# A sequence mixer and a gated MLP on one core: sines from SiLU's table, a product written with channels innermost, and a new order

## The chip, the cores and the metric

The kernel runs on one core of one Trainium2 chip. A core has TensorE (PE, matmuls into PSUM), VectorE (DVE), ScalarE (ACT), GpSimd (POOL) and SyncE (SP, which here issues DMA transfers); each takes its own list of instructions in order, and semaphores hold an instruction until what it needs is done. The metric is the time of one execution in device microseconds.

## The reference

Two branches read the same input `x` of 2048 positions by 512 channels, and a sigmoid gate per position mixes them. Branch A is a long convolution: its kernel K is made from 128 complex modes a channel, as exp(l dt A) weighted by C and dt B, summed over the modes; the reference convolves by FFT. Branch B is a gated MLP with hidden width 1792. All of it is float32.

```python
P = jnp.exp(logdA[:, :, None] * l[None, None, :])       # l = 0..2047
K = jnp.einsum("dn,dnl,dn->dl", Cc, P, dB).real
Kf, Uf = rfft2(pad(K)), rfft2(pad(u))                    # zero-padded to 2 L
y = irfft2(Uf * Kf)[..., :L] + u * Dskip                 # branch A
h = _sigmoid(x @ w_gate) * (x @ w_up)
b = h @ w_down                                           # branch B
g = _sigmoid((x * gate_w).sum(-1, keepdims=True))
return g * y + (1 - g) * b
```

## The kernel before

**Branch B.** `load_x`, `load_gu` and `load_dn` bring inputs and weights from HBM into staging tiles (`st`, later also `parts`, which are pieces of tiles that branch A no longer needs). `split` halves each value into two fp32r numbers: ACT copies the rounded upper part (L1031), DVE subtracts it to get the rest (L1032). `hidden` multiplies in 12 matmuls a product (three pairings of halves, four chunks of channels, tile `gups`, 128x512, L1098). `post` takes the sigmoid of the gate as a tanh on ACT (`sg`, L1141), multiplies on DVE (L1143), and splits the result again into `h` (L1147, L1148). `down` multiplies `h` with `w_down` (`dps`, L1170), and `add` scales a result on ACT (`part`, L1189) and accumulates it in HBM, through SP for the first and POOL for later groups. `gates` makes the mixing gate with a tanh of four columns (L727).

**Branch A, K.** For 16 groups of 32 channels, `angles` and `magnitudes` build a table `B` of 64 powers of each mode, and for eight pairs of groups `powers` and `tables` build a table `T` by doubling: five times, the last e entries times one power give the next e (L575 to L577, e = 1, 2, 4, 8, 16). Angles go through `trig`: ACT makes the rounded turn (L474), DVE subtracts it, ACT takes an absolute value (L478) and two sines (L479 with a bias column `hpi` for the cosine, L481). Magnitudes are exponentials on ACT (L504, L547, L549). Sine and exponential lie in different activation tables, so ACT loads a table (ACT_TABLE_LOAD, 1283 ns) whenever the kind turns; in the version before, tanh is in the exponential's table and not in the sine's. `tables` multiplies `T` and `B` (tile `kps`, L619), `sort` evicts that to `kst` on ACT (L627), DVE adds `Dskip`, and `second` multiplies with a Fourier matrix (`wps`, L649): 64 matmul calls, which the compiler makes 128 instructions of 128 columns, on tiles of 32 rows by 64 columns of the array, eight of which run side by side. `wps` fills two pairs of PSUM banks, and two ACT evictions (L658) write it to `kev`, whose rows hold 16 channels a frequency; SP stores `kev` to `a_k` in HBM (L661). Four pairs make one half of K (`a_k_60`, then `a_k_61`).

**Branch A, the rest.** `rows` folds `x` and transforms it (`ups`, evicted to `evu`, stored to `a_u`). When a half of K is stored, `passes` loads `a_u` and `a_k` back, `ustep` (`s2u`), `kstep` (`s2k`), `inverse` (`ips`, evicted to `ev`, stored to `b_s`) and `finals`/`last` (`fps`) finish the convolution, and POOL or DVE adds it to the output. Copies marked `either` may stand on ACT or DVE.

**The order.** Every function above is a generator that yields steps; `Plan.run` reads a string, `ORDER`, letter by letter, and each letter picks the next step of one kind on one engine, for `either` the engine too. So the string sets the order of all engines' lists. `Plan.cost` holds the durations that give slots and due times; it issues nothing. The two evictions of `second`, as they stand before, are:

```python
dst = kev.rearrange("p k (i u s) -> p u s i k", i=2, u=2)[:, u]
te = yield "ACT", 1.8, lambda: A.activation(dst, ph[u].rearrange("p j s i k -> p (j s) i k"), AF.Copy), [t, kvs.t]
```

They read 128 frequencies in a row from PSUM and write each 16 floats (64 bytes) after the one before.

Of the kernel before, what the change touches and what calls it, by code (L numbers as in the profile page):

```python
# [32 lines left out]
P = 128  # L33
# [32 lines left out]
ORDER = (  # L66
    "ABDdeEfgZZEfGDdBgeZZEfgDdeZGVEfZBgDdeZWZWEfpgZZFDEudWfgZZhepvpAuvEWfEgZZDfCHugZZHpqXDIDJvIFdeZuKFdeiuhadeZKZLZMKvivahZMZ"
    "MNOMMGPXVEfKMuNPviuaSZwSZxPSSSvuSSZSPYVSvSSuQgRSSaaZZaEZfvwZgZauaSaSvRQrtxHuEZQZQvQwZtZaaSuuENOZPaZfvSNxSSTfrYVgEutPwKvE"
    "tWWUZZPvGHffPoaKLMQgZZZgZEKppuvuMRWWfpFuZvZaEfRpqMvMgZaZQQQuMurQTNOwUPZZKNMSutSvShoaaSaPSPSivSSuSZZPwaaaZZuSrgQRESjkwlvg"
    "StaaxaESxFRESxmfxQZwZfhaQQivvugQtmZZFhExgSNOSuPfZZavvuNnviZSgaZFEEhPituvaSSPZTwyUPuoZaaXQaIaRJXVIKHKwyZaRQLafMKaafZguwyv"  # L70
    "gUaaZaMQMYVQQNfZaOZTMuMKrvtvPNMwyuvSgSSKSKrZtEEYZtVtWWPWSSWuvPoaaaaZSjkPLSQSfrtMKtwyaupSpSZRSvMSfRQQQSSQSggNaaZurawtMZMy"
    "lmamtaZaOawyZZuESvvaZFPNpSphiSTavXFEaPuauZwyZPUPQXvZuvRZRQQQhQuFTZMKZoZhEENOVYZZVHrFtutrUvtMSPNSoZtfgfgSjSfZuvSZSiigaPkS"
    "hvPYVaZSuWZSPuvQSRRviSaaZSpSQwynZrWutWErtEttWQSfSZagZvQpuaaQSpNpSOawylaaaaZmuPNwPyZSPfaaXaSTawyPmZXVZUQogIvZuaaaJIKKaYst"
    "tZRwyaaaaLMKRQQQQrNTOVMfvnMtHZMwyMKgYPNUotauMSSKSSPSZPSZrPaDDSDjtSakrluZtZKvQSRRvSZZaSvZSQtZmmQdtQuvDuQNOnbbbbbb0veSuZwa"
    "ayavZZZPuNdePFuP1bb2ZSSvShvuaSiSdPFZSTZLM3ewUy45uKMFdhohvvubeZZaZZQRR6bub4MbZbH5iavZqDia6QZbQQQNOTuZMMPDdwyUZ6NKvPvMSSSS"
    "oaaSSubDdeajSZPSkuPdlZ6Swaa7eZuQSSmabbmb8DdnyRveSeZv!RSZZvE0!$wa$ZuuSQQQQSNOS!!$$ESyZaaw1baaaP2ZZuNPSSTwUbv345vZyPEbvZfg"
    "PQoaaaZZuvR6bRIbJ4u6bIKQbZbuQKLMywZaQaa5fgwQKMZaaT6MvaNObyM67wZU8fMKPoavqyNMaaSKZSSSjkPZSgwEaFaKxaEGfSub!vSuZ!$$SPSSgbyw"
    "aaPZSuQZSaS!b!x$vvSRlZRQQuvufQQSZwamLMKaaZmuNEMhOf0Sw1b$b3MSxZPNMgSvaZxaaZ24SgvZ56bbEPPTb4wbUZPZQuMuZZboababRRu5Z6ZaivEv"
    "KQbZQZbEbQQTv6xNOEwU67fgx8ZuMnPfNoaufaaZSSSSvgS!uZSP!$$vSvPwaaSaZSZESPSQgFuvhixSjSfFuvZSRZRgZQuvS!hQkQ!FhlZiQiZufgwaaamv"
    "NamnZSwaaaOPNP$aESuvP$SST0wP1bbZyZxUQuvoRRQQQQZaa2fgaZaZTuvZ34ZwUoj5bEb66akuvbb4auvaZawlmmnbbbbZZZuvbab56aZZyfEug6bvbbbZ"  # L80
    "7b8E#u!Eb#b$b$bav#Zfgbawuv013344$Zaaa56$56b66bZbb9buZE9bZy90bZafwbb71bb3g9Zu24bay8!b!Z$ZEfvf#4v#g%$05b66bEaZbZuE5bbg6vbb"
    "b&($bbZ)bb)f((**(6(**gZ0Za199f22a99Z$ZwauFaugv193399a7fvuEFaZu8!#4Z9hvg4Z$!%u$i%#5F&(6))((**fZZEbvu$f(h6g$999g(w&))b5v**"
    "ZiZuZb4Zav)((*9%*((hy**FcZha667iZbu&()i5)((**ca((**bcbZazZcaa6avaz8!!!6$aaaazZc#v4Z566$aubauauy7Zaz8a!ya$v#u$c!av!aZzaav"
    "$$Zavu$azZu$999aaa9%ZZc&()aycZaZua9aFaF)v(v(**F999%&9h99u(9%&ia(*zvvu(h*vhiazia99aaaa()aaza)(a(az)z*99))c)%&a)c)cz(ca)a)"
    "z)c)*aaaa(a(a*z))acaazczc*")

# [90 lines left out]
class Plan:  # L177


    def __init__(self):  # L180
# [134 lines left out]
def body(ctx, tc, xp, xt, prm, ldt, dsk, gw, wgu, wdn, c_wu, c_wf, c_wk, c_wwk, c_wwu, c_wwv, c_pw, out):  # L315
# [115 lines left out]
    def preludes():  # L431

        yield E["dt"]
        for k in range(NG // NQ):
# [31 lines left out]
            quads[k][0].set(t)  # L466

    def trig(shape, f, cs, t):

# [8 lines left out]
        t = yield "ACT", act(n), lambda: A.activation(af, f, AF.Abs), [t]  # L478
        t = yield "ACT", ("sin", act(n) + 0.1), lambda: A.activation(cs, af, AF.Sin, scale=-2 * math.pi, bias=hpi), [t]  # L479
# [151 lines left out]
    def second(q, kss, kst, kready):  # L631
# [7 lines left out]
        banks = yield XB, 2  # L639
        ph = [b.tile("wps", [P, 2, 2, 2, P]) for b in banks]  # L640

        def mms():
            for i in range(2):
                for s in range(2):
                    for h in range(2):
                        for x in range(0, 4, 2):
                            for jj in range(4):
                                r = slice(32 * jj, 32 * jj + 32)
                                mm(ph[jj // 2][32 * x:32 * x + 64, jj % 2, s, i], kst[r, i, h, 4 * s + x:4 * s + x + 2], wk[r, h],  # L649
                                   start=(h == 0), stop=(h == 1), tile_position=(32 * jj, 32 * x), skip_group_check=True)  # L650
# [5 lines left out]
        for u in range(2):  # L656
            dst = kev.rearrange("p k (i u s) -> p u s i k", i=2, u=2)[:, u]
            te = yield "ACT", 1.8, lambda: A.activation(dst, ph[u].rearrange("p j s i k -> p (j s) i k"), AF.Copy), [t, kvs.t]  # L658
            banks[u].free(te)
# [59 lines left out]
    def gates(t4):  # L719
# [6 lines left out]
        def work():  # L726
            A.activation(g[:, c], gl[:, c], AF.Tanh, scale=0.5)  # L727
# [409 lines left out]
    def post(half, sb, f, pp):  # L1137
        (pg_, bg, tg), (pu, bu, tu) = pp
        ss, = yield SG, 1
        sg = ss.tile("sg")  # L1140
        t = yield "ACT", ("exp", actp(512)), lambda: A.activation(sg, pg_, AF.Tanh, scale=0.5), [tg, ss.t]  # L1141
        bg.free(t)
# [125 lines left out]
```

## Time and profile before

| | us |
|---|---|
| median of three runs | 648.88 |
| lowest and highest run | 645.97, 654.21 |
| profiled execution, its own time | 644.45 |
| span of that execution, first to last instruction | 642.7 |
| transfers of that execution | 105.50 MB, mean 164 GB/s |

In the profile an engine's busy time is the union of its instructions. Rows of waits say who waited for whom: engine, tile and line, the releaser, total, number and longest in microseconds. Rows of groups give the line, the operation, `out<-in` with shapes, the count, busy microseconds, the mean of one in ns, and idle time ahead. "PEld" are weight loads, which run beside matmuls. The chain of waits is the chain of work that ended last.

### The profile page before, as it was taken

To read this page: it belongs to the slowest core of one execution; us is meant where nothing else is said; L and a number is where in the kernel's file an instruction comes from. 1 tells how busy PE (TensorE), PEld (TensorE's weight loads), DVE (VectorE), ACT (ScalarE), POOL (GpSimd) and SP (SyncE) were. 2 spreads that over 40 slices of the span, in tenths; PEclk is the share of its full clock that TensorE was granted. 3 is DMA by queue.
4 is the path that set the end of the run, shared out by engine and by line. 5 is a ranking of instruction groups with operands and counts; after the bars stand their busy time and mean duration, and the time that the engine had idled before them with its cause. 6 is when DMAs were issued, how large, how long until landed. Compare 5 with 4: busy or idle time off the path is not lost.

```text
span 642.7 us, 16774 instructions
## 1 busy us (share of the span) xinstructions
PE 603.5 (94%) x7145; PEld 451.9 (70%) x7145; DVE 548.5 (85%) x784; ACT 431.3 (67%) x650; POOL 49.9 (8%) x61
## 2 busy tenths in 40 slices
PE   7999989899998997998999999989999987998987
PEld 3667778677876875866776777767776664676755
DVE  5999889999999999999999899998657652985367
ACT  4595998789898599789966899587642332442130
POOL 0000000011100110000010100000100010242021
PEclk9999999999999899899999999999999987999989
DMA  7504624439634628589488346735489999998986
GB/s 246 174 33 115 197 68 160 143 48 229 149 100 157 164 35 234 161 179 210 96 165 173 69 124 157 217 105 156 72 193 253 233 240 276 256 208 187 239 177 164
DMA packets 94650, 105.50 MB, mean 164 GB/s; under 512 B 39664, under 2 KB 65136, under 8 KB 93552
## 3 DMA queue, kind: packets, MB, share of 16 engines
q1 hardware_dynamic: 86512, 92.89, 53.1%
q0 software_dynamic: 8064, 11.54, 13.0%
q8 instruction: 56, 0.92, 0.6%
q14 instruction: 18, 0.15, 0.1%
HBM read 61.41 MB, written 42.99 MB: 162 GB/s over the span
## 4 chain that ended last, share of the span: by engine, by line
DVE 37%; PE 24%; ACT 14%; DMA 13%; issue 7%; SPq 4%; POOL 1%; DVEq 0%; POOLq 0%; ACTq 0%
PE gups L1098 10%; PE dps L1170 9%; DVE t L575 3%; DVE T L576 3%; DMA parts<-b_s 3%; DVE T L577 3%; DVE h L1148 2%; DVE sg L1143 2%; DVE gu L1032 2%; ACT B L547 2%; DMA parts<-a_u 2%; DVE B L556 2%; DMA st<-wgu 2%; DVE dnw L1032 2%; DVE ex L475 2%
## 5 line engine op out<-in xcount | busy, mean ns | idle before, releaser
L1098 PE MATMUL gups<-x,gu 128*128 128x512 f32 x1344 | 338.2, 399 | 5.7 <-ACT sg L1141 1.5
L1098 PEld LDWEIGHTS gups<-x,gu 128*128 128x128 f32 x1344 | 251.4, 190 | 77.3 <-issue 8.5
L1170 PE MATMUL dps<-dnw,h 128*128 128x512 f32 x672 | 176.8, 400 | 6.0 <-DVE h L1148 2.8
L1170 PEld LDWEIGHTS dps<-dnw,h 128*128 128x128 f32 x672 | 125.6, 190 | 45.2 <-issue 7.5
L1194 POOL DMA_DIRECT2D out<-part x31 | 27.8, 896 | 452.1 <-ACT part L1189 437.9
L1147 ACT ACTIVATE h<-sg 128x512 fp32r<-128x512 f32 x56 | 34.7, 627 | 32.7 <-DVE sg L1143 18.6
L547 ACT ACTIVATE B<-B 128x32 f32<-128x32 f32 (+2 forms) x96 | 53.5, 672 | 0.3
L1189 ACT ACTIVATE part<-dps,omg 128x512 f32<-128x512 f32 x47 | 32.0, 682 | 22.6 <-PE dps L1170 22.4
L1148 DVE TENSOR_TENSOR h<-sg,h 128x512 fp32r<-128x512 f32 x56 | 38.2, 684 | 7.6 <-ACT h L1147 7.5
L575 DVE TENSOR_TENSOR t<-T,bz 128x1024 f32<-128x1024 f32 (+3 forms) x48 | 41.2, 859 | 1.9 <-ACT ez L479 0.7
L577 DVE TENSOR_TENSOR T<-T,t 128x1024 f32<-128x1024 f32 (+3 forms) x48 | 41.5, 864 | 0.7
L1143 DVE SCALAR_TENSOR_TENSOR sg<-sg,gups 128x512 f32<-128x512 f32 x56 | 37.5, 679 | 5.3 <-ACT sg L1141 5.3
L576 DVE TENSOR_TENSOR T<-T,bz 128x1024 f32<-128x1024 f32 (+3 forms) x48 | 41.3, 860 | 0.0
L619 PEld LDWEIGHTS kps<-B,T 128*32 128x32 f32 x2048 | 29.4, 110 | 12.2 <-ACT part L1189 9.7
L1031 ACT ACTIVATE gu<-st 128x512 fp32r<-128x512 f32 (+1 forms) x49 | 29.1, 606 | 12.2 <-DMA st<-wgu 12.0
L619 PE MATMUL kps<-B,T 128*32 128x64 f32 x2048 | 31.9, 220 | 5.3 <-ACT part L1189 4.9
L1032 DVE TENSOR_TENSOR gu<-st,gu 128x512 fp32r<-128x512 f32 (+1 forms) x49 | 32.0, 661 | 3.0 <-ACT gu L1031 3.0
L1141 ACT ACTIVATE sg<-gups 128x512 f32<-128x512 f32 x56 | 33.1, 591 | 0.8 <-PE gups L1098 0.6
L658 ACT ACTIVATE kev<-wps 128x1024 f32<-128x1024 f32 x16 | 30.9, 2003 | 3.1 <-PE wps L649 3.1
L340 ACT ACTIVATE ev<-ips 128x512 f32<-128x512 f32 x23 | 13.2, 597 | 27.9 <-PE ips L879 19.9
L479 ACT ACT_TABLE_LOAD x23 | 29.5, 1283 | 0.4
L340 ACT ACTIVATE yt<-fps 128x512 f32<-128x512 f32 x7 | 4.2, 597 | 32.2 <-PE fps L954 32.2
(129 smaller groups left out, 728.7 us busy)
## 6 DMA issues: line engine op xcount, KB each, us to landing
st<-wgu SPq DMA_DIRECT2D x45, 256.0 KB, 4.8
a_u<-evu SPq DMA_DIRECT2D x32, 256.0 KB, 4.3
a_k<-kev SPq DMA_DIRECT2D x8, 1024.0 KB, 4.9
b_s<-ev SPq DMA_DIRECT2D x32, 256.0 KB, 4.4
out<-part POOLq DMA_DIRECT2D x31, 256.0 KB, 4.4
ak<-a_k SPq DMA_DIRECT2D x28, 256.0 KB, 6.1
parts<-b_s SPq DMA_DIRECT2D x24, 256.0 KB, 8.0
st<-wdn SPq DMA_DIRECT2D x23, 256.0 KB, 4.7
```

The costliest lines, as they stand in the source:

```text
L547: A.activation(B[:, :, 0, 1 << k::2 << k], B[:, :, 0, 1:64 >> k:2], AF.Exp, scale=float(1 << k))
L575: yield "DVE", c, lambda: V.tensor_tensor(t2, src, sb, op=OP.mult), [t, slot.t]
L576: te = yield "DVE", c, lambda: V.tensor_tensor(dst, src, br, op=OP.mult), [t]
L577: te = yield "DVE", c, lambda: V.tensor_tensor(dst, dst, t2[:, :, ::-1], op=OP.add), [te]
L619: mm(p[32 * jj:32 * jj + 32, s], T[:, 32 * i + ch, c], B[:, ch, c], start=(c == 0), stop=(c == 1), tile_position=(0, 32 * jj), skip_group_ ...
L1032: te = yield "DVE", dve(n), lambda: V.tensor_tensor(lo, st, hi.bitcast(F32), op=OP.subtract), [te]
L1098: mm(p, gu[:, a, k, dc], x[:, b, dc], start=(dc + n == 0), stop=(dc == NC - 1 and n == 2))
L1141: t = yield "ACT", ("exp", actp(512)), lambda: A.activation(sg, pg_, AF.Tanh, scale=0.5), [tg, ss.t]
L1143: t = yield "DVE", dve(512), lambda: V.scalar_tensor_tensor(sg, sg, 1.0, pu, op0=OP.add, op1=OP.mult), [t, tu]
L1147: t = yield "ACT", act(512), lambda: A.activation(h[:, 0], sg, AF.Copy), [t, hs.t]
L1148: t = yield "DVE", dve(512), lambda: V.tensor_tensor(h[:, 1], sg, h[:, 0].bitcast(F32), op=OP.subtract), [t]
L1170: mm(p, h[:, a, 128 * s:128 * s + 128], dn[:, b], start=(f == fs[0] and n == 0), stop=(f == fs[-1] and n == 2))
```

## The change

1. The sines: `sine` issues, when the plan has just turned to the sine's kind, a SiLU of one column into a new tile `lead`, so that the table loaded is SiLU's, and then the sine without a load of its own. Tanh lies in that table too, so `post` and `gates` no longer declare a kind, and a tanh follows either table.
2. `second` writes its product with the four values of a frequency (i, s) innermost: each matmul's 128 columns lie 4 floats apart in PSUM. The evictions read two neighbours (s) from one bank, two from the other (j), and write those four next to each other in `kev`.
3. `split` takes its size as an argument (512, or 256 for the first weights); the planner's durations for a table turn (1.48 with the SiLU), the evictions (1.0) and the tanh change.
4. `ORDER` is another string throughout.

```diff
-    "ABDdeEfgZZEfGDdBgeZZEfgDdeZGVEfZBgDdeZWZWEfpgZZFDEudWfgZZhepvpAuvEWfEgZZDfCHugZZHpqXDIDJvIFdeZuKFdeiuhadeZKZLZMKvivahZMZ"
+    "BAEfgBDdeZZEEfDdegZZBGDdeGVWfpgZZWEpfWgDdpeZZWApEXfgZZDdeDEfguvZuHdHIJvCIKEfgZKLEfZgZuZDdFhMKiaMMMZevuFXhVFeZMYVNOKvDdeZ"
...
+    lead = cst.tile([P, 1], F32, name="lead")
...
-            return n[1] + (1.28 if n[0] != self.kind else 0.0)
+            return n[1] + ((1.48 if n[0] == "sin" else 1.28) if n[0] != self.kind else 0.0)
...
-                        self.kind = m[0]
+                        self.turned, self.kind = m[0] != self.kind, m[0]
...
+    def sine(dst, src, **bias):
+        if plan.turned:
+            A.activation(lead, hpi, AF.Silu)
+        A.activation(dst, src, AF.Sin, scale=-2 * math.pi, **bias)
...
-        t = yield "ACT", ("sin", act(n) + 0.1), lambda: A.activation(cs, af, AF.Sin, scale=-2 * math.pi, bias=hpi), [t]
+        t = yield "ACT", ("sin", act(n) + 0.1), lambda: sine(cs, af, bias=hpi), [t]
...
-        t = yield "ACT", ("sin", act(n)), lambda: A.activation(f, f, AF.Sin, scale=-2 * math.pi), [t]
+        t = yield "ACT", ("sin", act(n)), lambda: sine(f, f), [t]
...
-        ph = [b.tile("wps", [P, 2, 2, 2, P]) for b in banks]
+        ph = [b.tile("wps", [P, 2, P, 2, 2]) for b in banks]
...
-                                mm(ph[jj // 2][32 * x:32 * x + 64, jj % 2, s, i], kst[r, i, h, 4 * s + x:4 * s + x + 2], wk[r, h],
+                                mm(ph[jj // 2][32 * x:32 * x + 64, jj % 2, :, i, s], kst[r, i, h, 4 * s + x:4 * s + x + 2], wk[r, h],
...
-            dst = kev.rearrange("p k (i u s) -> p u s i k", i=2, u=2)[:, u]
-            te = yield "ACT", 1.8, lambda: A.activation(dst, ph[u].rearrange("p j s i k -> p (j s) i k"), AF.Copy), [t, kvs.t]
+            dst = kev.rearrange("p k (i u j s) -> p u k i j s", i=2, u=2, j=2)[:, u]
+            te = yield "ACT", 1.0, lambda: A.activation(dst, ph[u].rearrange("p j k i s -> p k i j s"), AF.Copy), [t, kvs.t]
...
-        t1 = yield "ACT", ("exp", 0.6), work, te
+        t1 = yield "ACT", 0.6, work, te
...
-        t = yield "ACT", ("exp", actp(512)), lambda: A.activation(sg, pg_, AF.Tanh, scale=0.5), [tg, ss.t]
+        t = yield "ACT", actp(512), lambda: A.activation(sg, pg_, AF.Tanh, scale=0.5), [tg, ss.t]
```

Two places of the engines' lists show what the new string and the tables do. Line numbers of the changed kernel are six or seven higher below `sine`. The first is ACT, about the third of the four `gates`. Before:

```order
L1141 ACTIVATE sg<-gups 128x512
L479 ACT_TABLE_LOAD
L479 ACTIVATE ez<-af,hpi 128x384
L727 ACT_TABLE_LOAD
L727 ACTIVATE g<-gl 128x4
L728 ACTIVATE omg<-g 128x4
L729 ACTIVATE g<-g 128x4
L1141 ACTIVATE sg<-gups 128x512
L481 ACT_TABLE_LOAD
L481 ACTIVATE ez<-ez 128x384
L504 ACT_TABLE_LOAD
L504 ACTIVATE ey<-ey 128x320
```

The same stretch of work in the changed kernel (`ez` and its exponential `ey`, L511):

```order
L1147 ACTIVATE sg<-gups 128x512
L472 ACT_TABLE_LOAD
L472 ACTIVATE lead<-hpi 128x1
L473 ACTIVATE ex<-af,hpi 128x32x32
L481 ACTIVATE af<-ez 128x384
L473 ACTIVATE ex<-ex 128x32x32
L1195 ACTIVATE part<-dps,omg 128x512
L485 ACTIVATE af<-ez 128x384
L473 ACTIVATE ez<-af,hpi 128x384
L1037 ACTIVATE x<-st 128x512
L473 ACTIVATE ez<-ez 128x384
L511 ACT_TABLE_LOAD
```

Four loads stood among the sines of one `ez` and its exponential; now two stand there, and the sines of an `ex` and an `ez` share the first. Over the whole list it is 49 loads before and 43 now.

The second place is SP, from the last store of `kev` on, where the second half's loads begin. Before:

```order
L661 DMA a_k_61<-kev 128x2048
L775 DMA wwu<-c_wwu 128x256
L784 DMA parts<-a_u 64x4x256 x4
L791 DMA wwk<-c_wwk 128x256
L1028 DMA st<-wgu 128x512
L796 DMA ak<-a_k_61 64x16x64 x2
L791 DMA wwk<-c_wwk 128x256
L796 DMA ak<-a_k_61 64x16x64 x2
L1028 DMA st<-wgu 128x512
L1028 DMA parts<-wgu 128x512
```

In the changed kernel, from two weight loads ahead of that store:

```order
L1034 DMA st<-wgu 128x512 x2
L668 DMA a_k_61<-kev 128x2048
L782 DMA wwu<-c_wwu 128x256
L791 DMA au<-a_u 64x4x256 x2
L791 DMA parts<-a_u 64x4x256 x2
L798 DMA wwk<-c_wwk 128x256
L803 DMA parts<-a_k_61 64x16x64 x2
L798 DMA wwk<-c_wwk 128x256
L803 DMA ak<-a_k_61 64x16x64 x2
L906 DMA b_s_62<-ev 64x1024
```

Weight loads (`wgu`, 256 KB each) have moved from behind that store to ahead of it: to the end of the list nine follow it before, and four now.

More of the change, by code (lines that the diff above doesn't have):

```diff
@@ L71 @@
[L71 to L82, printed above, removed]
@@ new lines @@
+    "ZNSEvpSTfMpfuwUxgvfZpPHPrttuPQgvgZiuZZvZRRuEfpoaaqauZQQQgQTvNMvKZOwxfUrPNMSSuZoSvZSEPSjukavPSSSaZuvSPtaQZSgZuvlwxRZSaZaR"
+    "SZZmaQQuvSQQSZfwaaFaFtSEtuvZNhOimFSZPZNuvZguvhiSXSfPwZaPhiuavZEfaZZPSauTZwEfXVgUEQoYVIaayaaZZfuZErtntvJRIKgKLHRQMKtQQgQN"
+    "vgwaaaaMMOyZMwyaaaaTZMKfgPNuvwUruvxytMSSSSZYVZoEajatkSPZSWuvSaPKSSrtWKLWatEWPZZZruMSlQRSpRSwapSvKaQQQyQaaumfgNvSSpOMZwaZ"
+    "aaMaZmPwSNauvZEZaaayyFSExuZvZftShiPPSTFuvpwyXZFPMuhiUQMhivZoRRZZnEFXZVgQZfEfuvYVuZZvZaQuvhiQaurvQattuvTNgOafwytUgKPNMSSS"
@@ L87 @@
+    "a*)a)aaza)ac))z)czc((**azc")
 XLATE = 0
@@ L1057, in load_gu @@
                         src = wgu[f].rearrange("p (k c m) -> p k c m", k=2, c=NC)[:, :, k]
-                        yield from split("splitw", src, gu[:, 0, :, k], gu[:, 1, :, k], gs, ready)
+                        yield from split("splitw", src, gu[:, 0, :, k], gu[:, 1, :, k], gs, ready, 256)
                         if k == 0:
```

24 lines of the change are left out of this document (15 added, 9 removed).

## The prediction

> **What bounds the kernel now.** I read the head of the profile first, then the busy time of each engine in three stretches, and then what TensorE (PE) waited for in each of them, because PE is the engine with the largest share.
>
> ```profile
> span 642.7 us, 16774 instructions
> ...
> PE 603.5 (94%) x7145; PEld 451.9 (70%) x7145; DVE 548.5 (85%) x784; ACT 431.3 (67%) x650; POOL 49.9 (8%) x61
> ```
>
> The columns of the next rows are stretch, length, and the busy microseconds of PE, PE's weight loads, DVE, ACT and POOL, then granted clock, DMA share and GB/s.
>
> ```profile
> 0.00:60.00 60.00, 53.17 (x234) 36.66 (x235) 51.51 (x105) 37.27 (x62) 0.73 (x5) 1.00 0.42 132
> 60.00:500.00 440.00, 422.55 (x5626) 325.77 (x5625) 408.95 (x554) 350.77 (x508) 24.51 (x28) 0.99 0.60 151
> 500.00:642.70 142.70, 127.83 (x1289) 89.50 (x1287) 87.99 (x126) 43.22 (x80) 24.69 (x28) 0.95 0.98 218
> ```
>
> PE is idle for 642.7 - 603.5 = 39.2 us: 6.8 at the start, 17.5 in the long middle stage, 14.9 in the last stage. The middle stage is tight on two engines at once: PE has 17.5 us free of 440 and DVE 31. ACT has 89 us free there, so on average it bounds nothing. But a share is an average, and the waits say where it matters. In the middle stage (columns: total, times, longest):
>
> ```profile
> PE kps L619 <- ACT part L1189: 4.9, 4, 1.9
> PE dps L1170 <- DVE h L1148: 2.5, 2, 1.7
> PE wps L649 <- ACT evu L340: 2.0, 2, 1.4
> PE wps L649 <- ACT ev L340: 2.0, 2, 1.4
> PE gups L1098 <- ACT sg L1141: 1.3, 2, 0.9
> PE dps L1170 <- ACT kst L627: 1.2, 1, 1.2
> ```
>
> The four ACT rows that free a bank (part, evu, ev, kst) and the sigmoid row sum to 4.9 + 2.0 + 2.0 + 1.3 + 1.2 = 11.4 us. So 11.4 of PE's 17.5 idle microseconds in the middle stage end with an ACT instruction. They fall in places where ACT is full, such as 230 to 260 us, with ACT busy for 29.54 of 30:
>
> ```profile
> 230.00:260.00 30.00, 26.64 (x520) 20.08 (x519) 29.24 (x50) 29.54 (x45) 2.62 (x3) 0.95 0.60 158
> ```
>
> In the last stage PE waits for DMA instead:
>
> ```profile
> PE fps L954 <- DMA parts<-b_s: 5.2, 6, 2.6
> PE s2u L817 <- DMA parts<-a_u: 3.8, 5, 2.0
> PE s2k L844 <- ACT ev L340: 1.7, 1, 1.7
> ```
>
> So ACT time is worth something only where it stands ahead of PE, and no rearrangement can win more than PE's idle time.
>
> **Terms of the change on ACT.** The groups of ACT instructions, shapes apart (busy, mean ns):
>
> ```profile
> L658 ACT ACTIVATE kev<-wps 128x1024 f32<-128x1024 f32 x16 | 30.9, 2003 | 3.1 <-PE wps L649 3.1
> L479 ACT ACT_TABLE_LOAD x23 | 29.5, 1283 | 0.4
> L547 ACT ACTIVATE B<-B 128x512 f32<-128x512 f32 x16 | 19.1, 1192 | 0.0
> L340 ACT ACTIVATE evu<-ups 128x1024 f32<-128x1024 f32 x15 | 15.3, 1018 | 0.0
> L1031 ACT ACTIVATE x<-st 128x512 fp32r<-128x512 f32 x16 | 10.1, 630 | 5.1 <-DMA st<-xt 5.0
> L727 ACT ACTIVATE g<-gl 128x4 f32<-128x4 f32 x4 | 0.8, 200 | 1.1 <-DVE ju L714 1.0
> ```
>
> The eviction kev moves 1024 values from PSUM in 2003 ns, where evu moves as many in 1018. It writes single values 64 bytes apart. The L547 row with 512 values, written 16 bytes apart, shows the same price: 1192 ns against 630 for 512 contiguous values. The new form writes four neighbours (16 bytes) at a time. Its reads change too: two neighbours in one PSUM bank, then two in the other. For runs of two the nearest rows are the doubling steps on DVE:
>
> ```profile
> L340 DVE COPY ev<-ips 128x512 f32<-128x512 f32 x9 | 6.1, 688 | 9.8 <-PE ips L879 4.9 <-DMA out<-mn 3.0 <-ACT ev L340 1.8
> L340 DVE COPY uf<-s2u 128x1024 f32<-128x1024 f32 x4 | 4.9, 1217 | 0.0
> L576 DVE TENSOR_TENSOR T<-T,bz 128x256 f32<-128x256 f32 x8 | 3.4, 420 | 0.0
> L576 DVE TENSOR_TENSOR T<-T,bz 128x128 f32<-128x128 f32 x8 | 3.3, 407 | 0.0
> L459 DVE TENSOR_TENSOR pg<-pg 128x128 f32<-128x128 f32 x8 | 1.9, 283 | 0.0
> ```
>
> The first step has single values 128 bytes apart and costs 407 ns for 128 values, against 283 contiguous; the second has runs of two and costs 420 for twice as many. Runs of two carry no penalty there, in SBUF. I take kev at 1018 ns, and keep 2003 (reads from alternating banks as slow as the old writes) as the other end; better than 1018 is excluded, since 1018 is the contiguous copy. Term: 16 x (2003 - 1018) = 15.8 us less on ACT, or 0.
>
> Table loads: ACT's instruction list has 49 before and 43 after, because sigmoids and the gates no longer turn the table away from the sines. That is 6 x 1.283 = 7.7 us less. What one switch costs in all is seen where four loads follow one another:
>
> ```profile
> 292.71 0.57 ACT L1141 ACTIVATE sg<-gups 128x512 f32<-128x512 f32 x1
> 293.30 1.28 ACT L479 ACT_TABLE_LOAD   x1
> 294.59 0.62 ACT L479 ACTIVATE ez<-af,hpi 128x384 f32<-128x384 f32 x1
> 295.22 1.28 ACT L727 ACT_TABLE_LOAD   x1
> 296.51 0.20 ACT L727 ACTIVATE g<-gl 128x4 f32<-128x4 f32 x1
> ```
>
> From the end of the sigmoid (293.28) to the start of the sine (294.59) pass 1.31 us, of which the load is 1.28: nothing else is paid. The Trainium skill ("ScalarE: Activation LUTs", What ACT_TABLE_LOAD costs) adds a drain of about 1380 ns to each load, 2.66 us a switch; by it six fewer would give 16 us, an estimate, but this trace does not show the drain, so the sum stays with 1.28.
>
> Added: 21 one-column SiLUs (lead), each right behind a load. The nearest row is L727 with four columns, 200 ns: 21 x 0.20 = 4.2 us more, queued ahead of the sine and whatever ACT holds behind it. Copies that either engine may do have also moved: counted in the two lists, DVE gives up one evu, three s2u evictions and one ev, and takes two yt. That is 4 x 1.22 + 0.69 - 2 x 0.69 = 4.2 us off DVE, and about 4 x 1.02 - 0.6 = 3.5 us on ACT. The sines and the splits keep their work; the planner's numbers for them issue nothing.
>
> ACT in sum: -15.8 - 7.7 + 4.2 + 3.5 = -15.8 us. ACT is not the bound, so this is worth only what PE stops waiting. Between 0 (other instructions in front of the same evictions take over) and 11.4 I take 7: the ends of those waits lie in full stretches, where a load or a kev stands in front, but DVE is as full there (29.24 of 30 above) and is late next. The 4.2 us off DVE are counted in this 7, against the 2.5 us that PE waits for DVE's h.
>
> **PE.** The product wps now writes its 128 columns 16 bytes apart. No row of this trace has a matmul with a strided output. The chain of waits shows it gapless, and shows a mode change:
>
> ```profile
> 469.30 2.03 PE wps L649 x125
> ...
> 484.68 1.37 PE gups L1098 x6
> ...
> 486.73 1.42 PE s2u L817 x61
> 488.16 1.59 PE gups L1098 x6
> ```
>
> wps sends 128 instructions of 128 columns through eight tiles at once: 2048 columns in 2.03 us, 0.99 ns each. gups streams 6 x 512 columns in 1.37 us, 0.45 ns each. So in wps each column already has twice the time for its write. That is why I take 0; fewer than 0 is excluded, since the same columns still pass. The other end is ACT's doubling for 16-byte steps (1192 against 630, x 1.9): 2.03 x 0.9 = 1.8 us a product, 8 x 1.8 = 14.6 us. The cover is that slack per column; without it PE, the fullest engine, pays in full. The Trainium skill ("Advanced Engine Details and Errata", PSUM Cachelines) says that any non-contiguous PSUM pattern slows matmuls significantly and wants every two consecutive elements adjacent. By that rule the outer end would hold; no run here shows it yet.
>
> The new order goes 63 times from the large products to small ones, before 58. The first gups behind a small product takes 1.59 instead of 1.37, so five more returns cost 5 x 0.22 = 1.1 us.
>
> **The last stage.** The last a_k store leaves behind two kev evictions, so K's second half can start about 2 us earlier. And the queue SP has moved: after the last a_k store there were nine weight loads (wgu) still to issue, now four. They compete there with what PE waits for:
>
> ```profile
> 475.05 0.33 SPq L661 DMA_DIRECT2D a_k<-kev  x1
> 476.12 3.31 SPq L784 DMA_DIRECT2D parts<-a_u  x4
> 480.18 0.38 SPq L1028 DMA_DIRECT2D st<-wgu  x1
> ```
>
> ```profile
> 500.00:550.00 50.00, 43.62 (x571) 28.55 (x569) 25.39 (x34) 16.00 (x27) 3.54 (x4) 0.90 1.15 247
> ```
>
> Five loads of 256 KB are 1.3 MB, 5.3 us of transfer at 247 GB/s. PE's waits for transfers in the last stage are 5.2 + 3.8 = 9.0 us. The loads moved ahead run beside a middle stage at 0.60 DMA share, so they are hidden there; without that cover the 5.3 us come back. Between 0 and 5.3 I take 2, since the three PE waits for b_s and a_u have queues of their own in front. The number of POOL's accumulating stores is unchanged.
>
> **Sum.** -7 + 0 + 1.1 - 2 = -8 us, against the profiled execution's own 644.45 us (span 642.7 and 1.75 around it): 636.5. That execution lies 4.4 below the median of 648.88 (645.97 to 654.21). The change alone puts the median at 641. I take the middle, 639.
>
> **Rivals.**
> *The strided product is slow.* Place: the eight wps. Price 8 x 1.8 = 14.6 us, so 644.5 - 8 + 14.6 = 651, from the median 655.5. It turns the change slower than before from 1.0 us a product on, and slower by 2% (13 us) from (13 + 8) / 8 = 2.6 us on. For it: no row of a strided output; against it: 0.99 ns a column. Chance 0.15. The rule of the Trainium skill quoted above would give this case.
> *ACT's relief is hidden.* kev stays at 2003 because its reads now alternate banks, or DVE, full in the same stretches, takes over every wait. Then ACT gains nothing that PE sees: -2 + 1.1 = -1, 644 to 648. For it: ACT's 89 free us; against it: the 11.4 us of waits. Chance 0.17.
> *More than forecast.* The order closes all of PE's ACT waits and its DMA waits of the last stage: -11.4 - 9.0 - 1.7 + 1.1 = -21 us, 623.5 to 628, about 626; halfway to it, 632. Against it: the granted clock of 0.90 and the DMA share of 1.15 in 500 to 550 stay. Chance 0.17.
> The forecast, 633 to 646, has 0.51.
>
> **How the numbers follow.** The range, 629 to 655, leaves out the better half of the last rival and the worse half of the first. Faster by over 2% (below 636; about what a measurement of this kernel can tell from no change): 0.17 and a fifth of the forecast's 0.51, 0.27. Slower by over 2% (above 662): a third of the strided case and a little of the hidden one, where an order laid out for a short kev meets a long one, 0.09. Within: 0.64.
>
> **What would show it.** kev near 1.0 us and 43 loads of 1.28; a lead near 0.2; wps near 2.0 in the chain (3.8 for the first rival); PE's waits for part, evu, ev and kst below 5 us in the middle stage; fewer PE waits for b_s and a_u. I am wrong if wps is longer, if kev stays at 2, or if PE's idle time is still 39 us with the waits under new names.

## The result, and the profile after

| | before | changed |
|---|---|---|
| median, us (runs) | 648.93 (4) | 630.68 (4) |
| lowest to highest | 645.97 to 654.21 | 627.29 to 633.48 |
| profiled execution, us | 644.45 | 627.29 |
| PE idle in the span, us | 39.2 | 29.3 |

The ratio of the times is 0.971 (95% interval 0.962 to 0.979): the change makes the kernel about 3% faster. Of the kernels below, only the one with SiLU's table and the loads moved back had executions in a slower state, two of six (630.12 and 630.96 us): its median counts them, its ratio doesn't. The page of the changed kernel, its head:

```profile
span 625.5 us, 16787 instructions
...
PE 596.2 (95%) x7145; PEld 447.3 (72%) x7145; DVE 542.6 (87%) x781; ACT 414.4 (66%) x668; POOL 49.9 (8%) x61
```

To see where the time went, I cut both executions at the same event, the last store of `kev`, which stands at 475.05 us before and at 459.59 after. The first 60 us are the start, from there to the store is the middle stage, the rest is the last stage. Columns as in the prediction: stretch, length, busy PE, weight loads, DVE, ACT, POOL, then clock, DMA share, GB/s. Before:

```profile
60.00:475.05 415.05, 397.60 (x5323) 308.00 (x5322) 390.31 (x532) 345.18 (x499) 24.51 (x28) 0.99 0.57 144
475.05:642.70 167.65, 152.78 (x1591) 107.27 (x1589) 106.63 (x148) 48.81 (x90) 24.69 (x28) 0.96 0.99 225
```

And the changed kernel:

```profile
60.00:459.59 399.59, 391.69 (x5287) 304.83 (x5286) 383.68 (x527) 328.20 (x514) 24.51 (x28) 1.00 0.59 147
459.59:625.50 165.91, 151.26 (x1605) 105.25 (x1603) 106.49 (x147) 45.98 (x87) 24.66 (x28) 1.00 1.04 224
```

The middle stage is 415.05 - 399.59 = 15.5 us shorter, the last stage 1.7 us. In the middle stage DVE's busy time falls by 6.6 us and its idle time, length less busy, from 24.7 to 15.9. PE's idle time there falls from 17.5 to 7.9.

The groups of ACT's instructions of the changed kernel (busy, mean ns, idle ahead):

```profile
L665 ACT ACTIVATE kev<-wps 128x1024 f32<-128x1024 f32 x16 | 15.9, 1021 | 2.0 <-PE wps L656 2.0
L472 ACT ACT_TABLE_LOAD x21 | 26.9, 1283 | 0.4
L556 ACT ACT_TABLE_LOAD x14 | 18.0, 1283 | 0.3
L511 ACT ACT_TABLE_LOAD x7 | 9.0, 1283 | 0.1
L1037 ACT ACT_TABLE_LOAD x1 | 1.3, 1283 | 0.7 <-PEq L1261 0.7
L472 ACT ACTIVATE lead<-hpi 128x1 f32<-128x1 f32 x21 | 4.3, 203 | 0.2
```

`kev` has lost half its time, and the 43 loads are there. Note where they stand: 14 at L556, the first exponential that makes `B`; before, that line (L549 there) had four, and twelve stood at the sigmoids. PE's waits of the middle stage that end with ACT:

```profile
PE kps L626 <- ACT part L1195: 1.9, 3, 0.8
PE gups L1104 <- ACT sg L1147: 1.7, 1, 1.7
PE wps L656 <- ACT evu L340: 1.2, 1, 1.2
...
PE dps L1176 <- ACT part L1195: 0.7, 2, 0.5
```

They sum to 5.5 us. Before, all rows of this kind sum to 12.0 (the prediction's 11.4 leaves out two small ones). Everything that the prediction asked to see of ACT is here. That reading is consistent, and the experiments show that it is wrong.

### The profile page after: what moved, and what is told of

Same layout as the page of the kernel before. It is cut to its first block, busy times and chain, and to the rows that moved or that the text cites. A ratio compares the mean times of both kernels' runs of the same rounds, so it can differ in the third digit from the quotient of the medians.

```text
span 625.5 us, 16787 instructions
## 1 busy us (share of the span) xinstructions
PE 596.2 (95%) x7145; PEld 447.3 (72%) x7145; DVE 542.6 (87%) x781; ACT 414.4 (66%) x668; POOL 49.9 (8%) x61
## 4 chain that ended last, share of the span: by engine, by line
PE 36%; issue 23%; DVE 14%; DMA 14%; ACT 7%; SPq 3%; POOL 2%; POOLq 0%; DVEq 0%; ACTq 0%
PE gups L1104 18%; PE dps L1176 11%; DMA b_s<-ev 3%; PE kps L626 2%; POOL out L995 2%; DMA ak<-a_k 2%; ACT B L554 2%; DMA st<-wdn 2%; DMA st<-xt 2%; PE wps L656 1%; DMA parts<-b_s 1%; DVE T L583 1%; PE s2k L851 1%; DVE T L584 1%; DMA au<-a_u 1%
## 5 line engine op out<-in xcount | busy, mean ns | idle before, releaser
L1104 PEld LDWEIGHTS gups<-x,gu 128*128 128x128 f32 x1344 | 250.1, 189 | 77.9 <-issue 10.5
L1176 PEld LDWEIGHTS dps<-dnw,h 128*128 128x128 f32 x672 | 123.4, 188 | 43.3 <-issue 6.9
L1037 ACT ACTIVATE gu<-st 128x512 fp32r<-128x512 f32 (+1 forms) x49 | 29.3, 605 | 10.8 <-DMA st<-wgu 10.0
L626 PEld LDWEIGHTS kps<-B,T 128*32 128x32 f32 x2048 | 29.3, 110 | 8.6 <-ACT part L1195 4.2
L481 ACT ACTIVATE af<-ex 128x1024 int32<-128x1024 f32 x16 | 16.9, 1055 | 16.8 <-DVE ex L532 16.8
L559 DVE TENSOR_TENSOR B<-B,ex 128x1024 f32<-128x1024 f32 x16 | 19.6, 1224 | 9.1 <-ACT B L554 8.9
L472 ACT ACT_TABLE_LOAD x21 | 26.9, 1283 | 0.4
```

The source lines that it names most:

```text
L626: mm(p[32 * jj:32 * jj + 32, s], T[:, 32 * i + ch, c], B[:, ch, c], start=(c == 0), stop=(c == 1), tile_position=(0, 32 * jj), skip_group_ ...
L1104: mm(p, gu[:, a, k, dc], x[:, b, dc], start=(dc + n == 0), stop=(dc == NC - 1 and n == 2))
L1176: mm(p, h[:, a, 128 * s:128 * s + 128], dn[:, b], start=(f == fs[0] and n == 0), stop=(f == fs[-1] and n == 2))
```

## The experiments

**Which edit did it.** The change has three edits that can be made apart: the new `ORDER`, the product and eviction of `kev`, and the sines. (The planner's new numbers go with the edits they describe, and `split`'s size with the string; they issue nothing, but the planner's durations choose which staging tile a load takes.) Six kernels fill in the combinations between the kernel before and the changed one. One theory says that ACT's shorter work is what PE got; its rival says that the order did it.

*The new order alone*: the new string, with `wps`, `kev` and the sines as they were.

```diff
-    "ABDdeEfgZZEfGDdBgeZZEfgDdeZGVEfZBgDdeZWZWEfpgZZFDEudWfgZZhepvpAuvEWfEgZZDfCHugZZHpqXDIDJvIFdeZuKFdeiuhadeZKZLZMKvivahZMZ"
+    "BAEfgBDdeZZEEfDdegZZBGDdeGVWfpgZZWEpfWgDdpeZZWApEXfgZZDdeDEfguvZuHdHIJvCIKEfgZKLEfZgZuZDdFhMKiaMMMZevuFXhVFeZMYVNOKvDdeZ"
...
```

> The new order with the old sines (their own table, 45 loads) and the old wps and kev (2.0 us an eviction). Theory A (the two edits free ACT ahead of PE, in whichever order): the order alone keeps less than a third of the gain of 18 us, 640 to 648 us, since it was laid out for evictions of 1.0 us and PE waits for ACT again by 10 us or more in the middle stage. Theory B (the order does it, ACT's relief is hidden): 630 to 636 us, with PE's waits for ACT in the middle stage at 4 to 6 us as in the changed kernel.

*`kev` alone*, on the kernel before:

```diff
-        ph = [b.tile("wps", [P, 2, 2, 2, P]) for b in banks]
+        ph = [b.tile("wps", [P, 2, P, 2, 2]) for b in banks]
...
-            dst = kev.rearrange("p k (i u s) -> p u s i k", i=2, u=2)[:, u]
+            dst = kev.rearrange("p k (i u j s) -> p u k i j s", i=2, u=2, j=2)[:, u]
```

> The old order and sines, with only wps and kev in the new layout. All theories: kev near 1.02 us, wps about 2.05 us in the chain. Theory A: 16 us less on ACT take a good part of PE's waits for ACT away, 638 to 644 us. Theory B: 646 to 650 us, no change.

*The sines alone*, on the kernel before:

```diff
+        if plan.turned:
+            A.activation(lead, hpi, AF.Silu)
+        A.activation(dst, src, AF.Sin, scale=-2 * math.pi, **bias)
...
-        t = yield "ACT", ("exp", actp(512)), lambda: A.activation(sg, pg_, AF.Tanh, scale=0.5), [tg, ss.t]
+        t = yield "ACT", actp(512), lambda: A.activation(sg, pg_, AF.Tanh, scale=0.5), [tg, ss.t]
```

> The old order and kev, with only the sines on SiLU's table (45 loads before the order changes them, and as many leads as turns). ACT has 4 x 1.28 = 5.1 us less of loads and about 20 x 0.2 = 4 us more of leads. Theory A: 646 to 649 us, about nothing. Theory B: 646 to 650 us. A clear gain here would show that the place of a load matters (ahead of a sigmoid), not the sum.

*Both edits in the old order*: the two diffs above together.

> The old order with both edits. Theory A: most of the gain, 634 to 640 us. Theory B: 645 to 650 us. Theory C (a gap of PE costs more than its length, because the granted clock falls behind it): whatever gaps of 1.4 us or more go, the mean clock rises with them, and the time falls by about twice the idle time that goes.

*The changed kernel without the `kev` edit*:

```diff
-        ph = [b.tile("wps", [P, 2, P, 2, 2]) for b in banks]
+        ph = [b.tile("wps", [P, 2, 2, 2, P]) for b in banks]
...
-            dst = kev.rearrange("p k (i u j s) -> p u k i j s", i=2, u=2, j=2)[:, u]
+            dst = kev.rearrange("p k (i u s) -> p u s i k", i=2, u=2)[:, u]
```

> The changed kernel with the old wps and kev layout (2.0 us an eviction), new sines and order. Theory A: 16 us back on ACT give PE's waits for ACT back, 637 to 643 us. Theory B: 630 to 634 us.

*The changed kernel with the sines of before* (new order and new `kev`):

```diff
-        if plan.turned:
-            A.activation(lead, hpi, AF.Silu)
...
-        t = yield "ACT", actp(512), lambda: A.activation(sg, pg_, AF.Tanh, scale=0.5), [tg, ss.t]
+        t = yield "ACT", ("exp", actp(512)), lambda: A.activation(sg, pg_, AF.Tanh, scale=0.5), [tg, ss.t]
```

> The changed kernel with the old sines (45 loads, no leads), new kev and order. ACT's sum changes by 2 x 1.28 - 21 x 0.2 = -1.6 us, so by sums nothing: 629 to 634 us under both theories. If loads ahead of sigmoids are what PE waits for, 635 to 640 us.

Measured; the last columns are the middle stage and, in it, DVE's busy and idle time (all us):

| order, `kev`, sines | median | ratio to before (95%) | middle stage | DVE busy | DVE idle | last stage |
|---|---|---|---|---|---|---|
| old, old, old (before) | 648.93 | 1 | 415.05 | 390.31 | 24.74 | 167.65 |
| old, new, old | 644.12 | 0.993 (0.990 to 0.996) | 411.27 | 389.87 | 21.40 | 170.43 |
| old, old, new | 654.56 | 1.008 (1.005 to 1.011) | 417.85 | 390.33 | 27.52 | 174.05 |
| old, new, new | 651.96 | 1.004 (1.001 to 1.007) | 414.79 | 390.37 | 24.42 | 175.51 |
| new, old, old | 623.38 | 0.960 (0.955 to 0.964) | 397.74 | 382.60 | 15.14 | 164.36 |
| new, new, old | 619.45 | 0.954 (0.951 to 0.957) | 392.95 | 382.08 | 10.87 | 164.45 |
| new, old, new | 628.30 | 0.967 (0.963 to 0.971) | 404.60 | 383.13 | 21.47 | 166.40 |
| new, new, new (changed) | 630.68 | 0.971 (0.962 to 0.979) | 399.59 | 383.68 | 15.91 | 165.91 |

The rows of the middle stage behind three lines of the table. The new order alone:

```profile
60.00:457.74 397.74, 390.77 (x5291) 305.38 (x5290) 382.60 (x526) 342.21 (x495) 24.56 (x28) 1.00 0.58 148
```

New order and `kev`, old sines:

```profile
60.00:452.95 392.95, 388.64 (x5282) 304.12 (x5281) 382.08 (x526) 327.93 (x495) 24.51 (x28) 1.00 0.58 149
```

Both edits in the old order:

```profile
60.00:474.79 414.79, 394.07 (x5316) 304.68 (x5315) 390.37 (x532) 327.30 (x515) 24.57 (x28) 1.00 0.59 144
```

PE's waits for ACT in the middle stage, the largest rows: first with the order alone, then with both edits in the old order.

```profile
PE kps L619 <- ACT part L1188: 1.9, 3, 0.8
```

```profile
PE kps L626 <- ACT part L1196: 6.2, 6, 1.7
PE dps L1177 <- ACT part L1196: 2.8, 7, 1.0
```

All rows of this kind sum to 4.0 us with the order alone and to 16.4 with both edits in the old order, against 12.0 before. None of the six medians lies in a range that was set for it (`kev` alone misses one by 0.1 us): the order gave more than either theory allowed, and neither foresaw that the sines would cost time.

Three things follow. The order alone gives 4.0%, by the medians more than the whole change (the intervals, 0.955 to 0.964 and 0.962 to 0.979, still touch), with ACT as busy in the middle stage (342 us) as before (345). The theory of the prediction falls: ACT 18 us lighter in the old order (327.30 against 345.18) leaves the middle stage at 414.79, as long as before, and PE waits for ACT more, not less. The sines cost time in either order: 0.8% in the old one, and in the new one 6.6 to 6.9 us of middle stage (392.95 to 399.59; 397.74 to 404.60; by the medians 11.2 and 4.9). The `kev` edit is worth 0.7% in the old order. In the new one its worth is not settled: the profiled middle stages are 4.8 to 5.0 us shorter with it, but the medians fall by 3.9 us with the old sines and rise by 2.4 with the new ones, and in both pairs the intervals of the ratios overlap. (A stage comes from one execution: for the last pair, from the fastest of the four of the changed kernel and the slowest of the six without the `kev` edit.) The kernel without the sines' edit beats both the kernel before and the changed one, with an interval apart from either.

DVE's idle time shrinks and grows with the edits while its busy time hardly depends on anything but the order. PE's idle time moves as well (17.5 us before, 20.7 with both edits in the old order, 4.3 in the fastest version), so idle time alone doesn't say which of the two sets the length. Two questions stand: whether DVE really does, and what the sines do to it.

**Does DVE set the middle stage?** Two kernels add a known amount to the fastest version. The first makes a product for `B` on DVE twice in eight of the sixteen groups, 8 x 1.22 = 9.8 us; the second evicts `kst` on ACT twice, 16 x 0.59 = 9.4 us.

```diff
-            te = yield "DVE", dve(1024), lambda: V.tensor_tensor(
-                B[:, :, 0, 1::2], re[:, :, None].to_broadcast(sh), odd.to_broadcast(sh), op=OP.mult), [t]
+            te = yield "DVE", dve(1024), lambda: [V.tensor_tensor(
+                B[:, :, 0, 1::2], re[:, :, None].to_broadcast(sh), odd.to_broadcast(sh), op=OP.mult) for _ in range(2 - gi % 2)], [t]
```

> The kernel with the sines undone, and the product that begins B done twice in eight of 16 groups: 8 x 1.22 = 9.8 us more on DVE, all but one before the last K store. If DVE sets the length of the middle stage: 627 to 631 us. If PE or ACT does and DVE follows: 619 to 623 us.

```diff
-        t = yield "ACT", actp(512), lambda: A.activation(kst.rearrange("p h s l -> p s h l"), p.rearrange("p s (h l) -> p s h l", h=2), AF.Copy), [t, kss.t]
+        t = yield "ACT", actp(512), lambda: [A.activation(kst.rearrange("p h s l -> p s h l"), p.rearrange("p s (h l) -> p s h l", h=2), AF.Copy) for _ in range(2)], [t, kss.t]
```

> The kernel with the sines undone, and the eviction kst done twice: 16 x 0.59 = 9.4 us more on ACT, between a small product and what follows it. If ACT's 60 us of free time in the middle stage cover it: 619 to 622 us. If ACT stands in the chain there: 626 us or more.

The medians are 630.34 and 625.22, against 619.45. The middle stage with more DVE work:

```profile
60.00:463.51 403.51, 391.44 (x5287) 304.30 (x5286) 392.59 (x535) 329.54 (x497) 24.55 (x28) 1.00 0.57 146
```

And with more ACT work:

```profile
60.00:457.67 397.67, 390.35 (x5283) 304.21 (x5282) 382.88 (x526) 337.23 (x511) 24.55 (x28) 1.00 0.58 148
```

DVE's busy time in the stage rises by 10.5 us (9.6 over the span) and the stage by 10.6; DVE's idle time stays at 10.9. So in the fastest version DVE's microseconds pass into the length whole. ACT's pass by half: 9.3 us more work, 4.7 us more stage, of which 3.9 are new idle time of DVE. ACT matters where DVE waits for it. PE, idle for only 4.3 us of the fastest version's stage, wasn't tried in the same way, and no work was added to the kernel before. There the case is argued: with both edits in its order PE was busy for 3.5 us less of the stage (394.07 against 397.60), and the stage did not get shorter.

**How the sines cost time with fewer loads.** The changed kernel has 43 loads; with the old sines the new order has 45:

```profile
L479 ACT ACT_TABLE_LOAD x22 | 28.2, 1283 | 0.4
...
L1140 ACT ACT_TABLE_LOAD x14 | 18.0, 1283 | 0.2
...
L504 ACT ACT_TABLE_LOAD x5 | 6.4, 1283 | 0.0
...
L549 ACT ACT_TABLE_LOAD x3 | 3.8, 1283 | 0.1
```

The last of the 45 stands at L1030. Here 14 sigmoids (L1140) turn the table back and three exponentials of `B` do (L549); in the changed kernel no sigmoid does, and 14 exponentials. Those exponentials have DVE behind them, which multiplies `B` by the sines' result next. The rows of DVE's waits, of the changed kernel and then of the one with the old sines:

```profile
DVE B L559 <- ACT B L554: 8.9, 7, 3.6
```

```profile
DVE B L552 <- ACT B L547: 4.9, 5, 2.9
```

One such wait, group for group. In the changed kernel ACT's list reads (start, length, what):

```profile
127.86 0.31 ACT L453 ACTIVATE dt<-pp 128x128 int32<-128x128 f32 x1
128.19 1.28 ACT L556 ACT_TABLE_LOAD   x1
129.49 0.27 ACT L556 ACTIVATE B<-B 128x32 f32<-128x32 f32 x1
129.66 3.31 ACT L554 ACTIVATE B<-B 128x32 f32<-128x32 f32 x6
```

and DVE's:

```profile
130.82 0.49 DVE L506 TENSOR_TENSOR ey<-pp,pw 128x320 f32<-128x320 f32 x1
133.00 1.23 DVE L559 TENSOR_TENSOR B<-B,ex 128x1024 f32<-128x1024 f32 x1 [1.68 <-ACT B L554]
```

With the old sines the same places are:

```profile
118.18 1.28 ACT L1140 ACT_TABLE_LOAD   x1
119.48 0.60 ACT L1140 ACTIVATE sg<-gups 128x512 f32<-128x512 f32 x1
121.15 0.69 ACT L1188 ACTIVATE part<-dps,omg 128x512 f32<-128x512 f32 x1 [1.07 <-PE dps L1169]
...
126.86 0.32 ACT L452 ACTIVATE dt<-pp 128x128 int32<-128x128 f32 x1
127.06 0.27 ACT L549 ACTIVATE B<-B 128x32 f32<-128x32 f32 x1
127.21 3.37 ACT L547 ACTIVATE B<-B 128x32 f32<-128x32 f32 x6
```

```profile
129.81 0.48 DVE L499 TENSOR_TENSOR ey<-pp,pw 128x320 f32<-128x320 f32 x1
130.61 1.23 DVE L552 TENSOR_TENSOR B<-B,ex 128x1024 f32<-128x1024 f32 x1 [0.31 <-ACT B L547]
```

The exponentials' table was loaded 9 us earlier, ahead of a sigmoid, and ACT was idle for 1.07 us shortly behind it. In the changed kernel the load stands between DVE's product and the exponentials that DVE waits for, and DVE waits 1.68 instead of 0.31 us: 1.37 more, about one load. Over the stage this wait is 8.9 - 4.9 = 4.0 us longer, of 5.0 us more idle time of DVE.

Two kernels test whether it is the place, or rather the leads, SiLU's table, or the planner's choices. The first keeps SiLU's table and the leads, and adds a one-column exponential ahead of each sigmoid or gate that turned the table in the version with old sines, so the 45 loads stand where they stood there:

```diff
+    def back():
...
+        if plan.turned:
+            A.activation(lead, hpi, AF.Exp)
...
-        t = yield "ACT", ("exp", actp(512)), lambda: A.activation(sg, pg_, AF.Tanh, scale=0.5), [tg, ss.t]
+        t = yield "ACT", ("exp", actp(512)), lambda: (back(), A.activation(sg, pg_, AF.Tanh, scale=0.5)), [tg, ss.t]
```

> The kernel with the sines undone, but sines on SiLU's table (with leads), and a one-column exponential ahead of the sigmoids that turned the table there: 45 loads in the same places as with the sines undone, and 36 leads of 0.2 us. If the place of the load counts (ahead of the exponentials that DVE waits for, in the changed kernel): 619 to 624 us, with DVE's waits for B near 5 us. If the added one-column instructions or SiLU's table itself cost the time: 630 us or more.

The second is the changed kernel with its planner's numbers as they are, but without the lead. The loads return to the sigmoids, and nothing else differs from the version with old sines but which staging tile some loads use:

```diff
-        if plan.turned:
-            A.activation(lead, hpi, AF.Silu)
```

> The changed kernel with its planner untouched, but sines issued plainly: no lead, the sine's own table, 45 loads, which now stand ahead of sigmoids too. Its instructions are those of the kernel with the sines undone; only which of the staging tiles a load takes can differ, since the planner's durations choose them. If the sines and their loads cost the 11 us between that kernel (619.5) and the changed one (630.7): 617 to 622 us. If the choice of staging tiles does: 628 to 633 us.

The first takes 623.15 us (ratio 0.958, 0.952 to 0.965), the second 622.54 (0.960, 0.956 to 0.965). Their middle stages are 394.42 and 393.88 us, and the wait for `B` is 5.1 and 5.0 us. The row of the first:

```profile
60.00:454.42 394.42, 389.62 (x5283) 304.42 (x5282) 382.61 (x526) 331.13 (x528) 24.56 (x28) 1.00 0.60 149
```

With SiLU's table, 36 one-column instructions (21 in the changed kernel) and two loads more, the stage is 5.2 us shorter than the changed kernel's. The wait for `B` goes with the place: 8.9 and 8.8 us in the changed kernel with and without the `kev` edit, where 14 loads stand ahead of `B`'s exponentials, and 4.9 to 5.1 in the four kernels of the new order, without added work, that have them ahead of sigmoids. So the place of the loads is most of the cost, by the stages and the waits; the ratios of these two kernels alone would not settle it, for their intervals (to 0.965) just reach that of the changed kernel (from 0.962). The one-column instructions cost little (394.42 us against 392.95 and 393.88 without them). The staging tiles may account for up to 0.6% (0.954 against 0.960); those intervals overlap.

**The strided product.** One kernel leaves `wps` contiguous in PSUM and lets the eviction read single values 512 bytes apart there, with the same writes of four neighbours:

```diff
-        ph = [b.tile("wps", [P, 2, P, 2, 2]) for b in banks]
+        ph = [b.tile("wps", [P, 2, 2, 2, P]) for b in banks]
...
-            te = yield "ACT", 1.0, lambda: A.activation(dst, ph[u].rearrange("p j k i s -> p k i j s"), AF.Copy), [t, kvs.t]
+            te = yield "ACT", 1.0, lambda: A.activation(dst, ph[u].rearrange("p j s i k -> p k i j s"), AF.Copy), [t, kvs.t]
```

> The changed kernel, but wps is written contiguously as before, and the eviction reads single values 512 bytes apart in PSUM and writes the same runs of four. If the stride of the writes alone cost the second microsecond, kev takes 1.0 us here too and the time is 628 to 634 us. If strided reads of single values from PSUM cost the same, kev takes 1.9 to 2.1 us, and the time is that of the kernel with kev undone.

It takes 628.87 us (0.969, 0.965 to 0.974), as the changed kernel does. Its eviction, in the groups:

```profile
L665 ACT ACTIVATE kev<-wps 128x1024 f32<-128x1024 f32 x16 | 15.9, 1024 | 2.0 <-PE wps L656 2.0
```

So the halving of `kev` needed only the writes in runs of four; turning the product was not needed, and it cost nothing. The last `wps` in the chain of waits takes 2.09 us strided, in the changed kernel, and 2.10 contiguous, in this one:

```profile
455.51 2.09 PE wps L656 x125
```

```profile
457.02 2.10 PE wps L656 x124
```

**Strides and gaps by themselves.** The last kernel adds matmuls at the start whose result nobody uses: blocks of 24 with bf16 operands, 512 columns each, written contiguously, then 16 bytes apart, contiguously, 8 bytes apart, contiguously; then contiguous blocks after gaps of growing length.

```diff
+    every4 = spin.rearrange("p (a b) -> p b a", b=4)
+    every2 = spin.rearrange("p (a b) -> p b a", b=2)
+    for to in (spin, every4, spin, every2, spin):
+        for _ in range(24):
+            mm(to, warm[:, :P], warm, start=True, stop=True)
...
```

> The changed kernel with bf16 matmuls of 512 columns ahead: blocks of 24 written contiguously, 16 bytes apart, contiguously, 8 bytes apart, contiguously; then six blocks of 24, each behind 1 to 6 ACT evictions of the same bank (gaps of about 0.9 to 3.6 us). Strides: if TensorE pays for a strided output at full column rate, a matmul goes from 0.21 us to 0.4 us at 16 bytes; if not, all blocks take 24 x 0.215 = 5.2 us once warm. Gaps (theory C): behind a gap of more than some 1.4 us the first 3 to 4 us of matmuls run at half the clock, 1.5 to 2 us longer a block; behind shorter ones nothing is lost.

Stretches of 5 us inside the blocks, in the same columns (16 bytes apart, contiguous, 8 bytes apart, contiguous):

```profile
15.00:20.00 5.00, 4.78 (x12) 1.61 (x12) 0.00 (x0) 0.00 (x0) 0.00 (x0) 1.00 0.00 0
20.00:25.00 5.00, 5.00 (x24) 2.21 (x23) 0.00 (x0) 0.00 (x0) 0.00 (x0) 1.00 0.02 3
...
30.00:35.00 5.00, 4.78 (x13) 1.56 (x12) 0.00 (x0) 0.00 (x0) 0.00 (x0) 1.00 0.00 0
35.00:40.00 5.00, 5.00 (x23) 2.18 (x22) 0.00 (x0) 0.00 (x0) 0.00 (x0) 1.00 0.00 0
```

A contiguous block runs 24 matmuls in 5 us, a strided one 12 or 13, at a granted clock of 1.00 in each. In these blocks a stride halves the speed, to about 0.8 ns a column (12.5 matmuls of 512 columns in 5 us, an estimate). `wps`, which is float32 and takes 0.99 ns a column anyway, doesn't feel it; that this slack is why is likely, but no run varied it. The Trainium skill ("Advanced Engine Details and Errata", PSUM Cachelines) has non-contiguous PSUM patterns slow matmuls significantly: that agrees with the bf16 blocks and not with the product that this change strides. The gaps are read in the last section.

## Why the prediction was right or wrong

The median of 630.68 lies in the range, near its lower end; the likeliest class, within 2%, did not come. The sum of -8 us was reached by the wrong terms, and that the median stayed in the range is luck: by the medians it is made mainly of an order worth 26 us and sines that cost 11 in it (619.45 to 630.68), and the sum has neither.

- **Durations: right.** `kev` at 1021 ns (1018 forecast), a lead at 203, 43 loads at 1283 ns. The drain that the Trainium skill ("ScalarE: Activation LUTs", What ACT_TABLE_LOAD costs) adds to a load is not shown after either: above, `dt` ends at 127.86 + 0.31 = 128.17 and the first exponential starts at 129.49, 1.32 us later. ACT's sum was forecast at -15.8 and is 431.3 to 414.4, -16.9.
- **"worth 7 of the 11.4": the step that failed.** PE's waits for ACT did shrink by 6.5 (12.0 to 5.5), near the 7. But ACT's relief did not do it. With the same relief in the old order they grow to 16.4, and the middle stage stays as it was (414.79 against 415.05); with the new order and no relief they are 4.0. The relief of `kev` and the cost of the sines cancel there: -3.8 and +2.8 us alone.
- **"The 4.2 us off DVE are counted in this 7": the mis-sized term.** DVE's busy time in the middle stage fell by 6.6 us (5.9 over the span), and a microsecond of DVE was a microsecond of stage where work was added to the fastest version. The remaining 8.8 us are DVE's idle time. I read PE as the bound because its share was largest (94%). In the fastest version DVE's list decides; that it did in the kernel before, where it was busy for 94% of the middle stage (390.31 of 415.05), is argued and not shown.
- **"No rearrangement can win more than PE's idle time": wrong.** The span fell by 17.2 us and PE's idle time by 9.9. The other 7.3 are busy time of the same 7145 matmuls, and the granted clock is enough for it: 0.984 before and 0.995 after, and 603.5 x 0.984 / 0.995 = 596.8, against 596.2 measured. I had taken the low clock of the last stage as given; it went from 0.96 to 1.00. In the kernel before it falls behind waits of PE, as here, where PE is idle for 1.8 of 5 us and the next 5 us run at 0.74:

```profile
205.00:210.00 5.00, 3.19 (x12) 2.05 (x11) 5.00 (x7) 3.96 (x9) 0.00 (x0) 0.92 0.39 149
210.00:215.00 5.00, 5.00 (x18) 3.99 (x17) 5.00 (x7) 3.15 (x5) 0.87 (x1) 0.74 0.61 114
```

Whether the higher clock made part of the gain or only came with the shorter waits was not separated.

- **The order at +1.1: wrong in sign.** Alone it is worth 26 us in the medians of its own comparison (649.41 to 623.38). I priced it by what it issues, mode returns and copies moved, and not by the waits that it removes, for which I had no row.
- **Six loads fewer as a gain of 7.7 us on ACT: right on ACT, wrong for the kernel.** I had counted the loads and not asked in front of whom they stand. The Trainium skill ("ScalarE: Activation LUTs", Table sets: the hidden batching unit) advises batching by set to have fewer loads; here 43 loads took 630.68 us, and 45 in other places took 619.45 with the old sines and 623.15 with SiLU's table.
- **The strided product at 0: right**; the reason given, the slack per column, fits the bf16 blocks. The other end, +14.6, isn't there.
- **The last stage at -2: the size is right (-1.7), by luck.** PE's wait for `a_u` is gone, and that for `b_s` is down from 5.2 to 3.3, but others have come (the largest is for `parts`, from ACT), and PE's idle time there is 14.7 us after 14.9. What fell is PE's busy time, by 1.5 us, with the clock at 1.00 instead of 0.96:

```profile
PE fps L961 <- DMA parts<-b_s: 3.3, 5, 1.0
PE dps L1176 <- ACT parts L1195: 2.3, 1, 2.3
```

That the five weight loads did this is not shown: two of them are issued only 1.7 us ahead of the store, and with the old order the last stage was 2.8 to 7.9 us longer in the three kernels that only have an edit (167.65 against 170.43 to 175.51), and 1.7 us can't be told from that.

Of the rivals, "More than forecast" came nearest by its time: the profiled execution of 627.29 lies in its 623.5 to 628, and the median below its halfway mark of 632. Its mechanism, PE's waits all closed, is not what happened. What "ACT's relief is hidden" describes did happen with both edits in the old order: ACT's gain is lost there, in part to the sines.

What stays open: which letters of the string make the order faster, since no part of it was tried apart; why the last stage was longer in the three kernels with the old order and an edit (PE's busy time, at a clock of 0.93 to 0.95, is 1.5 to 3.9 us of the 2.8 to 7.9); what `kev`'s edit is worth in the new order; and the staging tiles.

## What to carry to other kernels

Where two engines are over 90% busy in a stage, the larger share doesn't say which one sets its length: add a known amount of work to each and see which passes through whole (here DVE's 10.5 us gave 10.6, ACT's 9.3 gave 4.7). A list of waits that shrinks as forecast proves nothing until the edit has been run alone, and an order has to be run alone too, for its worth is not in what it issues. A table load is to be judged by who waits behind it: in the place shown it cost about its whole 1.28 us ahead of the exponentials that DVE waits for, and ahead of the sigmoid, where ACT was idle for 1.07 us soon after, the trace shows no wait of DVE behind it. And PE's busy time is no constant: at a higher granted clock the same matmuls kept PE busy for 7.3 us less.

## What the runs showed of the hardware

ACT's reads of single values 512 bytes apart in PSUM cost nothing (1024 ns for 1024 values), while its writes 64 bytes apart in SBUF doubled the time (2003). Matmuls with bf16 operands lost half their speed at 8 bytes of stride just as at 16. Between dense blocks of such matmuls, gaps of PE up to 2.5 us cost nothing beyond their length; the timeline of the probe's last blocks (idle time ahead in brackets):

```profile
48.50 5.34 PE L390 MATMUL spin<-warm 128*128 128x512 bf16 x24 [1.28 <-ACT spin L388]
...
63.59 5.34 PE L390 MATMUL spin<-warm 128*128 128x512 bf16 x24 [2.51 <-ACT spin L388]
72.05 7.03 PE L390 MATMUL spin<-warm 128*128 128x512 bf16 x24 [3.12 <-ACT spin L388]
```

24 matmuls took 5.34 us after 2.51 us of idleness and 7.03 after 3.12, 1.69 more; each gap was tried once. The 1.4 us of theory C are not borne out there. But 2.5 us are no safe length in the kernel: before, the clock fell to 0.74 behind a wait of 1.70 us (`dps` for `h`, in the stretch from 205 us above). Which history of PE lets it fall was not tried.
